# TensorE's order in the first down projection of an attention and bilinear feed-forward kernel, taken from the source

## Chip, cores and metric

The kernel runs on one core of one Trainium2 chip, as one launch. The metric is the device time of that launch in microseconds (us), read as the median of several runs. TensorE (PE) does the matrix products, VectorE (DVE) and ScalarE (ACT) read PSUM and do the elementwise work, GpSimd (POOL) does a little of it, and SyncE (SP) and ScalarE issue the DMA transfers.

## What is computed

The reference computes attention with a causal window of 128 keys and a linear bias, joins the heads, and sends the result through a bilinear feed-forward block. q, k and v have 8 batches, 8 heads, 576 positions and 64 channels; the block's weights are 512 by 1536, twice, and 1536 by 512.

```
scores = scale * np.matmul(q, k.transpose(0, 1, 3, 2))
...
scores = np.where(mask, scores + bias[None], -1000000000.0)
attn = np.exp(scores - max) ; attn = attn / (sum + 1e-09)
attn_out = np.matmul(attn, v)
x = attn_out.transpose(0, 2, 1, 3).reshape(B * S, H * D)
a = x @ w_a
b = x @ w_b
return (a * b @ w_out)
```

## The kernel before, in words

The weights reach the core as 64-bit words and are turned into a pair of 16-bit tiles, a high part and a low part. Almost every product is made of three 16-bit products (high by high, high by low, low by high) in one PSUM bank. `up_weights` (lines 166 to 203) does this for w_a and w_b. `down_weights` (205 to 233) does it for w_out: `convert` (lines 132 to 135, DVE), a square and a sum, a scale, and at the end for each of the 12 row blocks f one ACT copy (line 231) and one DVE subtraction (line 232), which write the tile `wdn`. Both are generators, joined in the chain `weights`; each `next` emits one step.

The batches run in a pipeline: while PE does the feed-forward products of batch b, the attention of batch b + 1 is done in between. `attention()` (line 667) is a generator of seven sections for each of four head pairs, and `Pace.along` (line 987) calls its sections at a set rate along the feed-forward steps. In a pair's turn stand `scores` (line 369: products `sc_ps`, line 380 for batch 1 and 384 later; a DVE pass, line 388; an ACT exponential, line 389), `normalize` (393: ACT line 405 and DVE line 406 write the probabilities into the tile `phl`), `transpose_probs` (409: one transposing DMA on SP's queue, line 411, from `phl` to the tile `pT`), and one pair later `pv` (510: 42 products `x_ps`, line 507, from `pT` and `vhl`). `split_qk` (333) begins with a small product `qtot` (line 337) for the pair after. `phl` is one tile without copies, so the next `normalize` waits until the transposing DMA has read it.

The feed-forward of batch 0 is emitted in `first_batch` (1019). `first_up` (785) makes the 12 hidden blocks f, each of four `up_ps` groups that ACT (line 792) and DVE (line 794) empty. `first_down` (813) then makes the output. For the first half t = 0 of the tokens it goes through f, and for each f through the four output blocks e, with three products each (line 818) into four open PSUM banks `dn_ps`, one for each e. For t = 1 it goes through e, and through f inside. All the banks named `up_ps` and `dn_ps` come from a cycle of five (lines 57 to 62), so a bank can be written only when the one five places earlier in the cycle has been read.

What sets the order: the whole is built under a scheduler that puts each engine's instructions into an order of its own, by a forecast of when they are ready. An engine named in `tc.manual_schedule` is left out: its instructions keep the order in which the source emits them. For the first batch this holds for SP alone (line 1034). For batches 1 to 7 it holds for PE alone (line 1038).

Of the kernel before, what the change touches and what calls it, by code (L numbers as in the profile page):

```python
# [46 lines left out]
def attention_then_bilinear_ffn(ctx: ExitStack, tc: tile.TileContext, qT, kT, vP, w_a, w_b, w_out, rel, slopes2, outT):  # L47
# [11 lines left out]
    def bank(name):  # L59

        pl = next(banks)
        return pl.tile([P, 512], F32, tag="ef" if pl is ps_ef else "ch", name=name)
# [103 lines left out]
    def up_weights():  # L166

        sq, rest, hi, ps = {}, [], [], None  # L170
        for f in range(NF + 2):
            conv = convert(f) if f < NF else iter(())
            next(conv, None)
            n = f - 1
            if 0 <= n < NF:
                if n % 2 == 0:
                    ps = ps_at.tile([P, 512], F32, tag="at", name="wn_ps")
                up_norms(n, sq.pop(n), ps)
                if n + 3 < NF:
                    load_weights(n + 3, (w_a[n + 3], w_b[n + 3]), sp)  # L180
                else:
                    k = 2 * (n + 3 - NF)
                    load_weights(n + 3, (w_out[k], w_out[k + 1]), sp)
            yield
            next(conv, None)
            if rest:
                rest.pop(0)()
            if 0 <= n < NF and n % 2:
                up_scales(n // 2, ps)
                hi += [(k, m) for k in (n - 1, n) for m in range(2)]  # L190
            yield
            if hi:
                rest.append(split_up(*hi.pop(0)))
            yield
            if f < NF:
                sq[f] = squares(f)
            if hi:
                rest.append(split_up(*hi.pop(0)))
            if rest:
                rest.pop(0)()  # L200
            yield
        for _ in range(len(rest)):
            rest.pop(0)()
# [575 lines left out]
    states, started, first_reads, last_read, last_main, last_bias = {}, {"down": -1}, [None], [None], [None], [None]  # L779


    def new_hidden():
        return work.tile([P, 2, HT], F32, tag="rc", name="rc", bufs=3)

    def first_up(st, h):

        late = []
        hid = {}

        def keep(f, t, m, ps):  # L790
            if m == 0:
                act.copy(hid[f][:, t, :], ps[:, 0:HT])
            else:
                vec.scalar_tensor_tensor(out=hid[f][:, t, :], in0=hid[f][:, t, :], scalar=st.g, in1=ps[:, 0:HT], op0=ALU.mult, op1=ALU.mult)
                if t:
                    halve(hid.pop(f), f, h, pool if f >= NF // 2 else vec)

        for f in range(NF):
            hid[f] = new_hidden()
            for t in range(2):  # L800
                for m in range(2):
                    ps = bank("up_ps")
                    terms(ps, (f, 3 if m else 0), B12 if t else 0, True, False)
                    terms(ps, (f, 2 if m else 1), 2 if t else 1, False, True)
                    late.append((f, t, m, ps))
                    if len(late) > 2:
                        keep(*late.pop(0))
                    yield
        for x in late:
            keep(*x)  # L810
        yield

    def first_down(b, oi, h):

        started["down"] = b
        def products(ps, f, e, t):
            for n, (wi, hi) in enumerate(((0, 0), (0, 1), (1, 0))):
                pe.matmul(ps[:, 0:HT], wdn[:, f, wi, e * P:(e + 1) * P], h[:, f, t, hi, :], start=(f == 0 and n == 0), stop=(f == NF - 1 and n == 2))  # L818

        def out(ps, e, t, o):  # L820
            with tc.high_priority(offset=PRIO):
                if e % 2:
                    vec.tensor_scalar(out=o, in0=ps[:, 0:HT], scalar1=oi, scalar2=None, op0=ALU.mult)
                else:
                    last_main[0] = act.activation(o, ps[:, 0:HT], AF.Copy, scale=oi)
            act.dma_start(outT[e * P:(e + 1) * P, b * S + t * HT:b * S + (t + 1) * HT], o)

        pss = [bank("dn_ps") for _ in range(NE)]
        for f in range(NF):
            for e in range(NE):  # L830
                products(pss[e], f, e, 0)
            yield
        more = new_hidden()
        for e in range(NE):
            out(pss[e], e, 0, row() if e < 2 else more[:, e - 2, :])
        for e in range(NE):
            ps = bank("dn_ps")
            for f in range(NF):
                products(ps, f, e, 1)
                if f % 4 == 3:  # L840
                    yield
            out(ps, e, 1, row())

    def row():
        return work.tile([P, HT], F32, tag="row", name="row", bufs=2)
# [115 lines left out]
    def out_scale(st):  # L961

        oi = small.tile([P, 1], F32, tag="oi", name="oi")
        vec.tensor_scalar(out=oi, in0=st.g, scalar1=smin, scalar2=so, op0=ALU.mult, op1=ALU.mult)
        vec.tensor_scalar(out=oi, in0=oi, scalar1=st.sv, scalar2=st.sv, op0=ALU.mult, op1=ALU.mult)
        vec.reciprocal(oi, oi)
        return oi

    def weave(main, *sides):

        for n, _ in enumerate(main):
            for side, a, z, steps in sides:
                if a <= n < z:
                    for _ in range((n + 1 - a) * steps // (z - a) - (n - a) * steps // (z - a)):
                        next(side, None)
# [24 lines left out]
    weights = chain(up_weights(), down_weights())  # L1000
# [4 lines left out]
    h = hid.tile([P, NF, 2, 2, HT], F16, name="h")  # L1005
# [8 lines left out]
    att = Pace(attention())  # L1014
# [4 lines left out]
    def first_batch():  # L1019
        st = states[0]  # L1020
        weave(att.along(first_up(st, h), 49, 3.2), (weights, 0, 40, 50))
        weave(att.along(first_down(0, out_scale(st), h), 24, 5.15), (weights, 0, 12, 12))
        for _ in weights:
            pass

    def batch(b):
        plain, fast = ways[b]
        n = 4 * len(plain) + 7 * len(fast)
        weave(att.along(up(states[b], h, plain, fast), n, NPAIR * b + 4), *((spread, *x) for x in quota[b][0]))
        weave(att.along(down(b, out_scale(states[b]), h, plain + fast), 48, NPAIR * b + 6), *((spread, *x) for x in quota[b][1]))  # L1030
        if b + 1 < B:
            assert b + 1 in states

    with tc.manual_schedule(engines=SP):
        first_batch()


    with tc.manual_schedule(engines={mybir.EngineType.PE}):
        for b in range(1, B):
            batch(b)  # L1040

# [39 lines left out]
```

## Time and profile before

| | |
|---|---|
| median of 3 runs | 992.15 us (991.67 to 992.97) |
| the profiled execution's own time | 989.81 us |
| its span | 988.0 us |
| PE busy | 962.1 us (97%) |
| DVE, ACT, POOL busy | 669.0, 635.6, 255.3 us |
| first down projection's products (line 818) | 288, from 153.5 to 200.2 us |

The span is what the trace covers; the execution's own time is 1.8 us longer. In a row of the timeline the first number is the start, the second the length of the merged group, then engine, line, operation, written tile and read tiles, partitions by elements, and a count; brackets at the end give how long the engine stood idle before it and what released it. Matmuls overlap, so the rate of a group is read from the starts of the group and of the next one.

### The profile page before, as it was taken

To read this page: it belongs to the slowest core of one execution; us is meant where nothing else is said; L and a number is where in the kernel's file an instruction comes from. 1 tells how busy PE (TensorE), PEld (TensorE's weight loads), DVE (VectorE), ACT (ScalarE), POOL (GpSimd) and SP (SyncE) were. 2 spreads that over 40 slices of the span, in tenths; PEclk is the share of its full clock that TensorE was granted. 3 is DMA by queue.
4 is the path that set the end of the run, shared out by engine and by line. 5 is a ranking of instruction groups with operands and counts; after the bars stand their busy time and mean duration, and the time that the engine had idled before them with its cause. 6 is when DMAs were issued, how large, how long until landed. Compare 5 with 4: busy or idle time off the path is not lost.

```text
span 988.0 us, 23867 instructions
## 1 busy us (share of the span) xinstructions
PE 962.1 (97%) x9339; PEld 748.9 (76%) x9339; DVE 669.0 (68%) x1867; ACT 635.6 (64%) x1729; POOL 255.3 (26%) x309
## 2 busy tenths in 40 slices
PE   7899999999999999999999999999999999999998
PEld 5567777677777777777777777777777777877776
DVE  5979998668688657777778677757776576514520
ACT  5977769667676667766767766777667766413321
POOL 1211122032546313541225222211232012311100
PEclk8999999999999999999999999999999999999999
DMA  8434753664337234463345362373245432200001
GB/s 333 168 126 172 231 154 67 151 158 92 80 74 183 68 69 87 107 172 75 68 92 121 120 118 65 87 191 84 59 84 117 133 74 38 55 34 5 1 13 36
DMA packets 148432, 102.82 MB, mean 104 GB/s; under 512 B 120032, under 2 KB 128352, under 8 KB 147296
## 3 DMA queue, kind: packets, MB, share of 16 engines
q1 hardware_dynamic: 138816, 91.77, 38.2%
q10 hardware_dynamic: 9504, 9.54, 3.0%
q8 instruction: 73, 1.20, 0.5%
q14 instruction: 39, 0.32, 0.1%
HBM read 48.33 MB, written 9.44 MB: 58 GB/s over the span
## 4 chain that ended last, share of the span: by engine, by line
PE 69%; DVE 12%; ACT 7%; DMA 7%; issue 3%; POOL 1%; SPq 0%; ACTq 0%; DVEq 0%
PE ch L856 19%; PE dn_ps L952 18%; PE p L856 14%; PE up_ps L856 9%; PE x_ps L507 4%; DMA v<-in_vP 4%; PE sc_ps L384 3%; DVE phl L406 2%; PE dn_ps L818 2%; ACT t L389 1%; DVE wsum L135 1%; DVE xs L442 1%; ACT phl L405 1%; DVE wsum L134 1%; DMA qk<-in_kT 1%
## 5 line engine op out<-in xcount | busy, mean ns | idle before, releaser
L856 PEld LDWEIGHTS <-wup 128*128 128x128 f16 x3072 | 296.3, 98 | 82.0 <-issue 5.7
L952 PE MATMUL dn_ps<-h,wdn 128*128 128x288 f16 x2016 | 254.4, 286 | 0.0
L952 PEld LDWEIGHTS <-wdn 128*128 128x128 f16 x2016 | 193.9, 98 | 52.0 <-issue 0.2
L856 PE MATMUL up_ps<-xs,wup 128*128 128x288 f16 x1536 | 194.6, 286 | 1.1 <-ACT rc L867 0.8
L856 PEld LDWEIGHTS <-wsum 128*128 128x128 f16 x1152 | 111.7, 98 | 32.0 <-issue 2.5
L911 POOL TENSOR_TENSOR rc<-rc,row 128x288 f32<-128x288 f32 x64 | 62.3, 974 | 279.8 <-DVE row L909 263.9
L389 ACT ACTIVATE t<-t,mn 128x192 f32<-128x192 f32 (+2 forms) x252 | 107.2, 427 | 24.5 <-DVE mn L388 24.4
L856 PE MATMUL ch<-xs,wup 128*128 128x288 f16 x768 | 115.0, 286 | 0.5 <-ACT row L893 0.5
L856 PE MATMUL p<-xs,wup 128*128 128x288 f16 x768 | 115.1, 286 | 0.0
L406 DVE SCALAR_TENSOR_TENSOR phl<-t,rin,phl 128x192 f16<-128x192 f32 (+2 forms) x252 | 104.6, 454 | 15.3 <-ACT phl L405 15.1
L856 PE MATMUL ch<-xs,wsum 128*128 128x288 f16 x768 | 111.5, 286 | 1.1 <-ACT rc L881 1.1
L848 ACT CAST h<-rc 128x576 f16<-128x576 f32 x96 | 64.1, 668 | 69.1 <-DVE rc L916 37.2
L405 ACT ACTIVATE phl<-t,rin 128x192 f16<-128x192 f32 (+2 forms) x252 | 88.9, 425 | 25.3 <-DMA pT<-phl 12.7
L849 DVE TENSOR_TENSOR h<-rc,h 128x576 f16<-128x576 f32 x90 | 69.5, 772 | 30.5 <-ACT h L848 29.7
L388 DVE CUSTOM_DVE_ANT_0 t<-sc_ps,bias,neg 128x192 f32<-128x192 f32 (+2 forms) x216 | 73.9, 389 | 7.6 <-PE sc_ps L384 7.5
L957 ACT ACTIVATE row<-dn_ps,oi 128x288 f32<-128x288 f32 x56 | 27.6, 493 | 55.9 <-PE dn_ps L952 55.9
L893 ACT ACTIVATE row<-ch,g 128x288 f32<-128x288 f32 x64 | 31.8, 497 | 48.9 <-PE ch L856 48.9
L442 DVE TENSOR_TENSOR xs<-v,xs 128x576 f16<-128x576 f32 x52 | 47.8, 935 | 21.4 <-ACT xs L441 21.3
L888 DVE TENSOR_TENSOR rc<-p,rc 128x288 f32<-128x288 f32 x64 | 29.1, 454 | 44.3 <-PE p L856 34.7
L365 POOL TENSOR_SCALAR bias<-rel_sb,ninv,sl_sb 128x192 f32<-128x192 f32 x24 | 20.0, 832 | 147.8 <-DVE mn L388 129.8
L856 PE MATMUL p<-xs,wsum 128*128 128x288 f16 x384 | 57.5, 286 | 0.0
L436 POOL TENSOR_TENSOR xq<-xq,sq 128x576 bf16<-128x576 bf16 x22 | 29.2, 1325 | 75.7 <-ACT sq L435 75.7
(155 smaller groups left out, 1386.1 us busy)
## 6 DMA issues: line engine op xcount, KB each, us to landing
v<-in_vP SPq DMA_DIRECT2D x8, 1280.0 KB, 6.2
out<-row ACTq DMA_DIRECT2D x62, 144.0 KB, 1.8
qk<-in_qT SPq DMA_DIRECT2D x28, 288.0 KB, 4.0
qk<-in_kT SPq DMA_DIRECT2D x28, 288.0 KB, 4.4
wdn<-in_w_a SPq DMA_DIRECT2D x12, 512.0 KB, 5.1
wdn<-in_w_b SPq DMA_DIRECT2D x12, 512.0 KB, 6.1
wdn<-in_w_out SPq DMA_DIRECT2D x12, 512.0 KB, 4.6
qst<-qkh SPq DMA_DIRECT2D x24, 144.0 KB, 2.7
```

Of the source, the lines that this page charges most:

```text
L388: vec.tensor_tensor_reduce(out=t[:, c:c + w], in0=ps[:, c:c + w], in1=o.bias[:, WIN - w:WIN], scale=-0.125 if o.b == 1 else o.neg, scalar= ...
L389: act.activation(t[:, c:c + w], t[:, c:c + w], AF.Exp, bias=o.mn[:, n:n + 1], scale=-1.0, accum_out=o.sm[:, n:n + 1])
L405: act.activation(phl[:, 0, pc:pc + w], e, AF.Copy, scale=s)
L406: vec.scalar_tensor_tensor(out=phl[:, 1, pc:pc + w], in0=e, scalar=s, in1=phl[:, 0, pc:pc + w], op0=ALU.mult, op1=ALU.subtract)
L442: vec.tensor_tensor(out=xs[:, n, 1, :, :], in0=src, in1=xs[:, n, 0, :, :], op=ALU.subtract)
L507: last = pe.matmul(xp[oc // 512][64 * h:64 * h + 64, o0:o0 + w], vt[0:rows, c:c + 64], probs(pt, rows, blocks, h), start=(n == 0 and first ...
L848: act.copy(h[:, f, :, 0, :], hid)
L849: eng.tensor_tensor(out=h[:, f, :, 1, :], in0=hid, in1=h[:, f, :, 0, :], op=ALU.subtract)
L856: pe.matmul(ps[:, 0:HT], w[:, wi, k, :], xs[:, b, xi, k, :], start=(first and n == 0), stop=(last and n == len(ks) - 1), skip_group_check= ...
L893: last_read[0] = last_main[0] = act.activation(mid, ch, AF.Copy, scale=st.g)
L911: pool.tensor_tensor(out=x0, in0=x0, in1=mid, op=ALU.mult)
L952: pe.matmul(ps[:, 0:HT], wdn[:, f, wi, e * P:(e + 1) * P], h[:, f, t, hi, :], start=(m == 0 and n == 0), stop=(m == NF - 1 and n == 2))
```

## The change

The call of `first_down` is taken out of `first_batch`, where its steps and twelve steps of `weights` were woven together under the scheduler. What is left of `weights` is now emitted before it, and `first_down` is emitted after it, in the section in which PE's order is that of the source. The rate at which attention is called along it is the same. SP, which kept the source's order in this stage, is now ordered by the scheduler there.

```diff
     def first_batch():
         st = states[0]
         weave(att.along(first_up(st, h), 49, 3.2), (weights, 0, 40, 50))
-        weave(att.along(first_down(0, out_scale(st), h), 24, 5.15), (weights, 0, 12, 12))
         for _ in weights:
             pass
...
     with tc.manual_schedule(engines={mybir.EngineType.PE}):
+        for _ in att.along(first_down(0, out_scale(states[0]), h), 24, 5.15):
+            pass
         for b in range(1, B):
             batch(b)
```

No instruction is added or taken away; all engines keep their order up to the first product of `first_down`, and PE's order is the same again from the 2111th row of its program on. In between the rows move. The number behind a name tells apart the buffers of one tile name.

First place: PE, at the end of the first hidden block f = 0 of `first_down`. `dn_ps_2116` and `dn_ps_2117` are now the banks of output blocks e = 2 and e = 3. Now stands there:

```order
L818 MATMUL dn_ps_2116<-h_787,wdn_122 128x288
L818 LDWEIGHTS wdn_122
L818 MATMUL dn_ps_2117<-h_787,wdn_122 128x288 [waits Activation_49]
L818 LDWEIGHTS wdn_122
L818 MATMUL dn_ps_2117<-h_787,wdn_122 128x288
L818 LDWEIGHTS wdn_122
L818 MATMUL dn_ps_2117<-h_787,wdn_122 128x288
L337 LDWEIGHTS ones16_73 [waits DVE_49]
L337 MATMUL qtot_2142<-both_2042,ones16_73 128x2 [waits PE_49]
```

The fourth bank is opened by the tenth product of `first_down`, and a wait for ACT stands on it. Before, the fourth bank was called `dn_ps_2096`, and its first product stood here, behind 62 other products of `first_down`, `qtot` and eight score products:

```order
L818 MATMUL dn_ps_2094<-h_787,wdn_122 128x288
L818 LDWEIGHTS wdn_122
L818 MATMUL dn_ps_2095<-h_787,wdn_122 128x288
L818 LDWEIGHTS wdn_122
L818 MATMUL dn_ps_2095<-h_787,wdn_122 128x288
L818 LDWEIGHTS wdn_122
L818 MATMUL dn_ps_2096<-h_787,wdn_122 128x288 [waits Activation_49]
```

The same wait moved from the 63rd product of the stage to the 10th.

Second place: PE, at the first products of probabilities and values of the stage (pair 2 of batch 1; `pT_1991` is its transposed probabilities). Now:

```order
L818 LDWEIGHTS wdn_122
L818 MATMUL dn_ps_2117<-h_787,wdn_122 128x288
L380 MATMUL sc_ps_2166<-qkl_1463,qkh_1462 64x192 x4
L507 LDWEIGHTS vhl_2086
L507 MATMUL x_ps_2176<-pT_1991,vhl_2086 64x128 [waits DMAHW4_49]
```

Before:

```order
L818 LDWEIGHTS wdn_122
L818 MATMUL dn_ps_2095<-h_787,wdn_122 128x288
L818 LDWEIGHTS wdn_122
L818 MATMUL dn_ps_2095<-h_787,wdn_122 128x288
L507 LDWEIGHTS vhl_2086
L507 MATMUL x_ps_2157<-pT_1991,vhl_2086 64x128 [waits DMAHW4_49]
```

Of the products of `first_down`, 104 stood ahead of this wait for the transposing DMA before, and 24 stand ahead of it now. The score products `sc_ps_2166` were ahead of it in both.

Third place: ACT, from the last copies of `wdn` in its block of ten on; this is one piece of the difference. The row `L792` is ACT's last reading of an `up_ps` bank, and `L326` is the sum of squares that waits for a load of q and k.

```order
 L792 COPY rc<-up_ps 128x288
-L231 ACTIVATE wdn<-wsum,ratio 128x512
-L389 ACTIVATE t,sm<-t,mn 128x192 x2
-L435 ACTIVATE sq<-v 128x576
-L231 ACTIVATE wdn<-wsum,ratio 128x512
+L389 ACTIVATE t,sm<-t,mn 128x192 x2
+L435 ACTIVATE sq<-v 128x576
+L231 ACTIVATE wdn<-wsum,ratio 128x512 x2
```

Everything up to `L792` stands as it did, ten copies of `wdn` among it, and the two copies left come a little later. Further down, `L326` of the next pair moves ahead of four copies into `phl` (line 405), and the four squares of the next values (line 282) stand in one block. On DVE too the last two `phl` rows of pair 2 (line 406) have the same ten subtractions of line 232 ahead of them. On SP the load of the next values (line 273) moves ahead of a transposing DMA and of two moves of q and k (lines 354 and 355).

## The prediction

> **What bounds the kernel now.** The page comes first: which engine fills the span.
>
> ```profile
> span 988.0 us, 23867 instructions
> PE 962.1 (97%) x9339; PEld 748.9 (76%) x9339; DVE 669.0 (68%) x1867; ACT 635.6 (64%) x1729; POOL 255.3 (26%) x309
> ```
>
> PE is busy for 97% of the span; the whole span holds 25.9 us in which it is not. The change takes no work from PE, so it can win only idle time, and it can lose any amount. The second view is the table by stretches of time around the first down projection (columns: us, then busy time of PE, PEld, DVE, ACT, POOL, then clock, DMA share, GB/s).
>
> ```profile
> 125.00:150.00 25.00, 21.41 (x235) 16.67 (x233) 23.79 (x56) 18.61 (x50) 6.55 (x4) 1.00 0.56 148
> 150.00:175.00 25.00, 24.80 (x252) 18.60 (x253) 21.49 (x69) 22.29 (x57) 4.78 (x5) 1.00 0.40 85
> 175.00:200.00 25.00, 22.57 (x237) 17.55 (x235) 13.15 (x46) 14.28 (x42) 1.78 (x2) 1.00 0.71 148
> 200.00:225.00 25.00, 24.15 (x224) 18.86 (x222) 16.80 (x60) 17.86 (x55) 10.31 (x16) 1.00 0.55 140
> 350.00:988.00 638.00, 631.33 (x6076) 496.61 (x6073) 394.33 (x1119) 383.23 (x1039) 154.58 (x161) 1.00 0.36 80
> ```
>
> From 150 to 175 PE is idle for 0.2 us, from 175 to 200 for 2.4. The third view, PE's waits from 140 to 400 us (total, times, longest), names them:
>
> ```profile
> PE wtot L103 <- DVE c L102: 2.4, 1, 2.4
> PE x_ps L507 <- DMA pT<-phl: 2.4, 1, 2.4
> PE sc_ps L380 <- issue: 1.4, 1, 1.4
> PE sc_ps L384 <- DVE mn L388: 1.2, 2, 0.8
> PE qtot L337 <- DVE both L329: 1.2, 1, 1.2
> PE up_ps L856 <- ACT rc L867: 0.8, 1, 0.8
> ```
>
> The waits of `wtot` and of the 1.4 us stand ahead of the first down product, where no engine's order changes. So the stage to be reordered holds one wait, 2.4 us for a transposed `pT`. The fourth view is PE's timeline of that stage:
>
> ```profile
> 153.47 0.90 PE L818 MATMUL dn_ps<-h,wdn 128*128 128x288 f16 x6
> 154.30 0.87 PE L380 MATMUL sc_ps<-qkl,qkh 64*64 64x192 f32 x8
> 155.10 4.22 PE L818 MATMUL dn_ps<-h,wdn 128*128 128x288 f16 x33
> 159.16 0.17 PE L337 MATMUL qtot<-both,ones 128*128 128x2 bf16 x1
> 160.32 7.89 PE L818 MATMUL dn_ps<-h,wdn 128*128 128x288 f16 x63
> 168.14 1.54 PE L507 MATMUL x_ps<-pT,vhl 128*64 128x128 f16 x42
> 169.61 0.87 PE L380 MATMUL sc_ps<-qkl,qkh 64*64 64x192 f32 x8
> ...
> 183.93 0.25 PE L507 MATMUL x_ps<-pT,vhl 128*64 128x128 f16 x2 [2.44 <-DMA pT<-phl]
> ```
>
> Up to 168.14 PE never stands still here: the scheduler has 104 down products ready to fill with. A down product takes 0.125 us (7.82 us from 160.32 to 168.14, by 63), a group of eight score products 0.80 (154.30 to 155.10). What the first `x_ps` and the fourth bank wait for is on the other engines' timelines, ACT, then DVE, then SP, and in the DMA view from 160 to 168 us (last number: us from issue to landing):
>
> ```profile
> 158.17 0.79 ACT L405 ACTIVATE phl<-t,rin 128x192 f16<-128x192 f32 x2
> 160.02 0.38 ACT L792 COPY rc<-up_ps 128x288 f32<-128x288 f32 x1
> 167.46 0.64 ACT L405 ACTIVATE phl<-t,rin 128x64 f16<-128x64 f32 x2 [0.63 <-DMA pT<-phl]
> ```
> ```profile
> 159.84 0.74 DVE L406 SCALAR_TENSOR_TENSOR phl<-t,rin,phl 128x192 f16<-128x192 f32 x2
> ```
> ```profile
> 160.65 4.84 SPq L411 DMA_TRANSPOSE pT<-phl  x1
> ```
> ```profile
> pT<-phl SPq DMA_TRANSPOSE x1, 6.7
> ```
>
> The last `phl` row ends near 160.6, the transposing DMA is issued at 160.65 and lands 6.7 us later, at 167.4. Before, `x_ps` stood at 168.14, just behind it.
>
> **The change part by part.** No instruction comes or goes, and PE's order is new only from 153.47 us to the `qtot` ahead of the second `x_ps`. Three moves have a price.
>
> *The fourth bank, opened by the tenth product.* With five banks in a cycle, the one for e = 3 held the third `up_ps` group of f = 11, and ACT reads it in the L792 row that ends at 160.40. ACT's rows up to there are the same and wait for nothing that PE now does later, so it still ends at 160.40. PE reaches that product at 153.47 + 9 x 0.125 + 0.80 = 155.4 and stands for 5.0 us. Queued behind it is everything on PE.
>
> *`x_ps` of pair 2, moved ahead of 80 down products.* By its place PE would reach it after 24 down products and two score groups: 153.47 + 24 x 0.125 + 2 x 0.80 = 158.1. Its `pT` lands at 167.4. The stall up to there is 9.3 us, and the 5.0 of the fourth bank lie inside it: from 160.4 PE has 15 products left, `qtot` and a score group, 2.8 us, so it stands again from 163.2 to 167.4. Both ends of the DMA rest on ACT's L405 and DVE's L406; ahead of these the order shows the same ten copies and ten subtractions of `wdn`, so the "work on w_out above" moves neither. Term: +9.3.
>
> *The second `x_ps`.* From 153.47 to 183.93 PE did 30.46 - 2.44 = 28.0 us of work, and it is the same work now; PE comes there at 153.47 + 28.0 + 9.3 = 190.8. Is its `pT` there by then?
>
> ```profile
> 176.86 1.16 ACT L326 ACTIVATE qkl<-qk 128x1152 bf16<-128x1152 f32 x1 [2.72 <-DMA qk<-in_kT]
> ```
> ```profile
> 174.65 9.23 DMA pT<-phl
> ```
>
> The first row is ACT's timeline, the second the chain that ended last. ACT's L326 is now queued ahead of four L405 copies of pair 3, and it waits for a load. If that load is as late as before, ACT is through with L326 at 178.0, with four copies at 0.4 (two took 0.79) at 179.6; DVE is half a microsecond behind, and with 9.2 for the DMA `pT` is there near 189.4. That is ahead of 190.8, so the old wait of 2.4 goes: -2.4. Together: +6.9.
>
> *The clock.* Two idle times of 5.0 and 4.2 us with 2.8 us of work between are longer than any that this stage had. What the trace shows of such holes is at its start, and at the two waits of 2.4 (stretches of 3.41 us, laid on the clock's own changes; the first number behind the comma is PE's busy time, the clock stands third from the end):
>
> ```profile
> 8.82:12.23 3.41, 1.45 (x10) 0.73 (x8) 3.17 (x11) 2.17 (x8) 0.07 (x1) 1.00 0.99 404
> 12.23:15.64 3.41, 2.59 (x32) 2.12 (x34) 1.30 (x3) 3.41 (x10) 1.20 (x1) 0.50 1.03 407
> 22.47:25.88 3.41, 1.89 (x16) 0.96 (x14) 3.41 (x13) 2.46 (x8) 0.00 (x0) 1.00 0.94 330
> 25.88:29.29 3.41, 3.41 (x23) 2.68 (x24) 2.83 (x7) 2.15 (x8) 2.21 (x3) 0.50 0.78 284
> 141.92:145.34 3.42, 1.96 (x16) 1.33 (x14) 3.03 (x4) 1.24 (x3) 1.28 (x1) 1.00 0.19 42
> 179.47:182.88 3.41, 2.02 (x21) 1.32 (x19) 0.97 (x8) 1.60 (x7) 0.00 (x0) 1.00 1.08 259
> ```
>
> A stretch with 1.45 or 1.89 us busy was followed by one at a granted clock of 0.50; those with 1.96 and 2.02 were not. An idle time of 5.0 us leaves some stretch at least 2.5 us empty, under 0.9 busy, so the clock should fall. At 0.50 the 2.8 us of work between the stalls take at most 5.6 and still end before 167.4: nothing lost there. What counts is the half clock left at 167.4: none at best, at worst one stretch nearly whole and a second (the one from 12.23, at 0.50 with 2.59 busy, was followed by another at 0.50): 0 to 3.1 us lost, since half of the time at 0.50 is lost. I take 1.5, near half of one stretch, as the place of the stretches is not known. Term: +1.5.
>
> The Trainium skill ("TensorE: Matmul & The Clock Gate", section "What's actually happening") says that the clock halves after a window of about 3.4 us that is idle, and that the windows run freely. By that rule, taken to the letter, 5.0 us need not hold a whole empty window, the clock would mostly stay, and the sum would lack this term. The rows here show falls after stretches 42 and 55% busy, so I go by the rows.
>
> *Behind the stage.*
>
> ```profile
> 215.49 6.04 PE L856 MATMUL up_ps<-xs,wup 128*128 128x288 f16 x48 [0.85 <-ACT rc L867]
> ```
> ```profile
> 202.12 0.58 SPq L273 DMA_DIRECT2D v<-in_vP  x1
> ```
> ```profile
> 208.40 0.74 ACT L282 ACTIVATE vsq<-v 128x640 bf16<-128x640 f32 x1 [1.71 <-DMA v<-in_vP]
> ```
>
> ACT was late at 215.49 because its squares of `v` (L282) stood among its other rows and waited for a load until 208.40, 6.3 us after its issue. Now the load is issued ahead of a transposing DMA and the squares stand in one block, early beside a PE that comes some 8 us later: -0.9, with nothing as the other end. Its own price: the load is now ahead of two moves of q and k (L354, L355) that score products need.
>
> ```profile
> 189.63 2.44 DMA qst<-qkl
> ```
>
> From the score products that set these moves free to the ones that need them stand 72 down products, 9.0 us; the load's 6.3 and a move's 2.4 make 8.7, with two issues and a second move up to some 10.5. So it costs 0 to 1.5; I take 0. The other waits behind (1.2 of `qtot`, 1.2 of `sc_ps`) have the same order around them and stay; at best they go.
>
> Sum: +9.3 - 2.4 + 1.5 - 0.9 = +7.5 us. The profiled execution took 989.81 (span 988.0), so 997.3; the median of the runs is 992.15, 2.3 above it, and with the same shift the median is 999.7 us.
>
> **Rivals.**
>
> *Given back later.* The chain of attention is 2 to 4 us ahead of PE after the stage, so all later waits of the list could shrink: 2.4 for `qtot` and `sc_ps` beside the 0.9, and no clock loss: 9.3 - 2.4 - 0.9 - 2.4 = +3.6, 995.8. For it: those waits are on DVE and ACT. Against: they come after 60 us and more of a pipeline that PE's own order times. Chance 0.10.
>
> *The clock stays at 1.00*, as it did over the two holes of 2.4: +6.0, 998.2. Chance 0.20. By the page of the Trainium skill named above, taken to the letter, this is the likely course.
>
> *A new wait behind.* The half clock takes its full 3.1 and the moves of q and k come late by 1.5: +10.6, 1002.8. Chance 0.12.
>
> *Not slower.* The copies and subtractions of `wdn` emitted above let ACT and DVE reach L792, L405 and L406 earlier than the rows of before say, and `pT` lands by 160.5 instead of 167.4. Then `x_ps` costs at most 2.4, the later wait goes, and the sum is zero or a little under it: 992.1 to 990. It decides at 160.5: the DMA would have to be issued by 153.8, 6.9 us earlier. Against it: the same ten copies stand ahead of these rows on ACT, which is busy for 22.29 of the 25 us from 150 on. Chance 0.05. That the order does not change is excluded by its rows.
>
> **How the numbers follow.** The forecast has the remaining 0.53, at 999.7. The range reaches from the first rival's 995.8 to 1003.0, just above the third's: outside are the not-slower case and ends of two bounds at once. A measurement of this kernel tells about 0.2%, 2 us, from no change; every case but the last is above that. Faster 0.02, same 0.03, slower 0.95.
>
> **What would show it.** Right: PE's timeline with a wait of some 5 us on the tenth down product for ACT's `rc`, one of 1.5 to 4 us on `x_ps` for the DMA to `pT` near 167.4, no wait on the next `x_ps`, and a clock of 0.50 somewhere between 158 and 171. Wrong: `x_ps` starts before 164; or the second `x_ps` still waits; or the sum of PE's idle time grows by less than 4 us. If the clock's row reads 1.00 throughout, the term of 1.5 is wrong and the rest may stand.

## The result, and the profile after

The changed kernel takes 998.77 us (median of 7 runs, 997.49 to 1002.27) against 992.15 for the kernel before (7 runs, 989.50 to 995.00): a ratio of 1.007, 95% interval 1.0048 to 1.0093. It is slower by 0.7%, which lies within the forecast range; the forecast was 999.7. The profiled execution took 1000.83 us with a span of 998.9 at a mean granted clock of 0.988; that of before had 989.81, 988.0 and 0.995. So the two traces stand 11.0 us apart and the medians 6.6. Part of what follows is about that gap.

The page first, of the changed kernel.

```profile
span 998.9 us, 23865 instructions
PE 967.2 (97%) x9339; PEld 752.8 (75%) x9339; DVE 671.5 (67%) x1867; ACT 636.8 (64%) x1729; POOL 255.7 (26%) x309
```

PE does the same 9339 products and is busy 5.1 us longer with them; the rest of the 10.9 us by which the span grew is idle time. Work that lasts longer without having grown points at the clock. The table by stretches, with the columns of the prediction, says where:

```profile
150.00:175.00 25.00, 17.71 (x168) 12.74 (x163) 20.73 (x59) 20.00 (x51) 4.73 (x4) 0.85 0.42 89
175.00:200.00 25.00, 25.00 (x258) 19.74 (x257) 12.62 (x47) 15.19 (x44) 2.29 (x3) 1.00 0.49 113
200.00:225.00 25.00, 22.91 (x197) 17.47 (x195) 15.46 (x56) 15.83 (x50) 4.97 (x6) 0.93 0.75 170
```

From 150 to 175 PE had 252 products before and has 168 now, and its clock fell from 1.00 to 0.85. From 175 to 200 it makes up the 2.4 us of the old wait. From 200 to 225 it loses again, 27 products fewer at 0.93, in a stretch for which the forecast had a small gain. PE's waits from 140 to 400 us name the causes:

```profile
PE dn_ps L818 <- ACT rc L792: 4.8, 1, 4.8
PE x_ps L507 <- DMA pT<-phl: 2.5, 1, 2.5
PE wtot L103 <- DVE c L102: 2.5, 1, 2.5
PE sc_ps L384 <- DMA qkh<-qkh: 1.6, 1, 1.6
...
PE sc_ps L384 <- DMA qkl<-qkl: 0.5, 1, 0.5
```

The first two are the predicted stalls. The last two, score products that wait for moved q and k, are new, and the 0.8 for `up_ps` is gone. In PE's timeline:

```profile
153.66 0.41 PE L818 MATMUL dn_ps<-h,wdn 128*128 128x288 f16 x2
...
160.61 0.84 PE L818 MATMUL dn_ps<-h,wdn 128*128 128x288 f16 x3 [4.78 <-ACT rc L792]
161.24 0.21 PE L337 MATMUL qtot<-both,ones 128*128 128x2 bf16 x1
161.31 2.98 PE L818 MATMUL dn_ps<-h,wdn 128*128 128x288 f16 x12
164.22 0.87 PE L380 MATMUL sc_ps<-qkl,qkh 64*64 64x192 f32 x8
167.59 2.77 PE L507 MATMUL x_ps<-pT,vhl 128*64 128x128 f16 x42 [2.50 <-DMA pT<-phl]
...
191.98 1.51 PE L507 MATMUL x_ps<-pT,vhl 128*64 128x128 f16 x42
...
207.80 0.22 PE L384 MATMUL sc_ps<-qkh,qst 128*64 128x64 f16 x2 [1.64 <-DMA qkh<-qkh]
208.47 0.27 PE L384 MATMUL sc_ps<-qkl,qst 128*64 128x64 f16 x2 [0.45 <-DMA qkl<-qkl]
...
240.77 1.54 PE L507 MATMUL x_ps<-pT,vhl 128*64 128x128 f16 x42
```

The same third `x_ps` in the timeline of before:

```profile
229.81 1.54 PE L507 MATMUL x_ps<-pT,vhl 128*64 128x128 f16 x42
```

Three distances hold the whole difference between the two traces. From the first down product to the second `x_ps`: 30.46 us before (153.47 to 183.93), 38.32 now. From there to the third `x_ps`: 45.88 before, 48.79 now. From the third `x_ps` to the end of the span: 758.2 and 758.1. So all of it lies in these two parts, +7.86 and +2.91, and nothing is won or lost behind 240 us. The experiments are read by the same two distances.

### The profile page after: what moved, and what is told of

Its sections match the earlier page's. It is cut to its first block, busy times and chain, and to the rows that moved or that the text cites. A ratio compares the mean times of both kernels' runs of the same rounds, so it can differ in the third digit from the quotient of the medians.

```text
span 998.9 us, 23865 instructions
## 1 busy us (share of the span) xinstructions
PE 967.2 (97%) x9339; PEld 752.8 (75%) x9339; DVE 671.5 (67%) x1867; ACT 636.8 (64%) x1729; POOL 255.7 (26%) x309
## 4 chain that ended last, share of the span: by engine, by line
PE 73%; DVE 11%; ACT 7%; DMA 5%; issue 2%; POOL 0%; ACTq 0%; SPq 0%; DVEq 0%
PE ch L856 19%; PE dn_ps L952 18%; PE p L856 14%; PE up_ps L856 12%; PE x_ps L507 4%; PE sc_ps L384 3%; PE dn_ps L818 3%; DVE phl L406 2%; DMA v<-in_vP 1%; ACT phl L405 1%; DVE wsum L135 1%; ACT t L389 1%; DVE xs L442 1%; DVE wsum L134 1%; DVE t L388 1%
## 5 line engine op out<-in xcount | busy, mean ns | idle before, releaser
L405 ACT ACTIVATE phl<-t,rin 128x192 f16<-128x192 f32 (+2 forms) x252 | 88.7, 425 | 23.4 <-DMA pT<-phl 10.6
```

The source lines that it names most:

```text
L405: act.activation(phl[:, 0, pc:pc + w], e, AF.Copy, scale=s)
```

## The experiments

**Theory.** TensorE's order costs two nested stalls and the fall of the clock that they bring; the later waits come from SP, which the change also hands to the scheduler. **Rivals:** the work on w_out that now stands above; the new waits coming from PE's late place; the clock alone; and the attention sections standing at wrong places rather than the order as such.

All runs in one table: the ratio of the run's times to those of the kernel before on the same chip, with its 95% interval (the ratio of the two medians can differ from it by 0.001), and the two distances in the run's own trace.

| run | ratio | first down product to second `x_ps` | second to third `x_ps` | both |
|---|---|---|---|---|
| before | 1 | 30.46 | 45.88 | 76.34 |
| changed | 1.0070 [1.0048, 1.0093] | 38.32 | 48.79 | 87.11 |
| changed again (e7) | 1.0080 [1.0062, 1.0099] | 38.38 | 48.84 | 87.22 |
| e1, weights above only | 1.0001 [0.9988, 1.0013] | 30.39 | 45.57 | 75.96 |
| e2, SP by source too | 1.0061 [1.0044, 1.0079] | 38.11 | 44.84 | 82.95 |
| e9, e2 with squares behind `phl` | 1.0057 [1.0039, 1.0075] | 38.38 | 44.85 | 83.23 |
| e3, fourth bank late | 1.0097 [1.0074, 1.0121] | 40.91 | 48.87 | 89.78 |
| e6, warm | 1.0076 [1.0057, 1.0094] | 37.14 | 50.38 | 87.52 |
| e11, warm and SP by source | 1.0056 [1.0039, 1.0073] | 36.92 | 45.36 | 82.28 |
| e4, attention late | 1.0157 [1.0140, 1.0173] | 38.68 | 52.40 | 91.08 |
| e5, sections placed by hand | 1.0090 [1.0074, 1.0107] | 36.09 | 50.12 | 86.21 |
| e8, e5 with squares behind `phl` | 1.0050 [1.0033, 1.0067] | 32.92 | 49.80 | 82.72 |
| e10, before with a later second `x_ps` | 1.0012 [0.9997, 1.0027] | 31.03 | 47.67 | 78.70 |

In e4, e5, e8 and e10 the second `x_ps` stands behind another number of products, so for these only the last column can be set beside the others. In e5 and e8 even that needs a correction: 24 products of `up_ps` more than elsewhere stand ahead of their third `x_ps`, 3.0 us at 0.125 each. Less these, e5 has 83.2 and e8 79.7.

**e1: the half of the change that moves the weights' work.** PE stays under the scheduler, and the steps of `weights` stand above `first_down`.

```diff
-        weave(att.along(first_down(0, out_scale(st), h), 24, 5.15), (weights, 0, 12, 12))
         for _ in weights:
             pass
+        for _ in att.along(first_down(0, out_scale(st), h), 24, 5.15):
+            pass
```

> One part of the change alone: the work on w_out's words stands above the first down projection in the source, and PE's order there is left to the scheduler as before. The instructions of all engines then stand in the order of the kernel before, row for row. Theory (the price is PE's order): 1.000 of before, within 0.2%. Rival (the weights above delay something): there is no row by which it could. Besides, its profile is a second look at the program of before: the mean granted clock of most executions of before was 0.991 to 0.993, below the 0.995 of the profiled one, so a stretch at 0.50 behind one or both of the 2.4 us waits is expected, with 1 to 3 us more than the profiled execution of before.

Measured: 991.79 us against 991.30, and a stage that is 0.4 us off that of before. In the traces of both, the instructions of every engine have the same order. So this half of the change does nothing by itself, and the first rival falls. The run is also twelve more executions of what is before's program, and its profiled one was 2.6 us longer than before's, with one stretch of half clock more. That stretch did not come where it was expected, behind a wait of 2.4 us (the clock of e1 reads 1.00 from 125 to 200 us), but early. From 40 to 60 us, in before and then in e1:

```profile
40.00:60.00 20.00, 17.80 (x223) 12.03 (x220) 18.15 (x43) 17.95 (x49) 4.37 (x9) 1.00 0.16 55
```
```profile
40.00:60.00 20.00, 17.79 (x193) 11.74 (x193) 18.82 (x45) 17.39 (x49) 4.72 (x10) 0.91 0.24 89
```

The busy time is the same, 30 products fewer are done. One such stretch (3.41 us at 0.50) costs up to 1.7 us, by estimate half of its length, and lowers the mean clock by 0.0017. So it explains at most 1.7 of the 2.6 us.

**e2: SP keeps the source's order too.** In its trace SP has the order of before, and PE that of the changed kernel. ACT and DVE, which the scheduler orders, still differ from before in some places, and from the changed kernel in others.

```diff
-    with tc.manual_schedule(engines={mybir.EngineType.PE}):
+    with tc.manual_schedule(engines={mybir.EngineType.PE, mybir.EngineType.SP}):
         for _ in att.along(first_down(0, out_scale(states[0]), h), 24, 5.15):
             pass
+    with tc.manual_schedule(engines={mybir.EngineType.PE}):
         for b in range(1, B):
```

> The changed kernel, with SyncE's queue too in the source's order during the first down projection, so that the next values are loaded behind the two moves of q and k and the transposing DMA, as in the kernel before. Theory (most of the time is PE standing at two early waits): the waits of 4.8 us on the fourth bank and on x_ps until pT lands near 167.6 stay as in the changed kernel, and x_ps of pair 3 starts near 192; only the wait of 1.6 + 0.5 us for qkh and qkl at 207.8 goes, with the half clock behind it of up to 1.7 us. So 2 to 4 us less than the changed kernel, and in place of that the old 0.85 us at up_ps may come back: about 995 to 997.5 us, 1.003 to 1.006 of before. Rival (SyncE's order is what costs the time): back to 992, 1.000 of before, and the two early waits shrink.

Measured: 996.55 us. PE's waits from 140 to 300 us in e2:

```profile
PE dn_ps L818 <- ACT rc L792: 4.7, 1, 4.7
PE wtot L103 <- DVE c L102: 3.0, 1, 3.0
PE x_ps L507 <- DMA pT<-phl: 2.7, 1, 2.7
PE sc_ps L384 <- DVE mn L388: 0.4, 1, 0.4
```

Both predicted stalls stay; the waits for moved q and k are gone, with the same PE order. So those are not PE's late place, but SP's order. In SP's timeline of the changed kernel the load of v stands ahead of two moves, and the DMA view from 195 to 215 us (last number: us from issue to landing) shows what that does:

```profile
198.27 0.53 SPq L273 DMA_DIRECT2D v<-in_vP  x1
199.42 0.46 SPq L354 DMA_DIRECT2D qkh<-qkh  x1
200.23 0.46 SPq L355 DMA_DIRECT2D qkl<-qkl  x1
```
```profile
v<-in_vP SPq DMA_DIRECT2D x1, 1280.0 KB, 9.0
...
qkh<-qkh SPq DMA_DIRECT2D x1, 144.0 KB, 8.2
qkl<-qkl SPq DMA_DIRECT2D x1, 144.0 KB, 8.2
```

In e2 the load is issued at 210.06, behind the transposing DMA, as it is behind it in before; there, from 185 to 200 us, the same two moves took

```profile
qkh<-qkh SPq DMA_DIRECT2D x1, 144.0 KB, 2.9
qkl<-qkl SPq DMA_DIRECT2D x1, 144.0 KB, 3.5
```

That SP's order makes these waits is shown; that it is the load of v within it is read from these rows. In the traces of e3, e6 and e7, which have the load at the same place, the two moves took 7.4 to 8.3 us. SP's share is 4 us in the traces (87.11 and 87.22 against 82.95 and 83.23). By the ratios it is 0.9 to 2.3 us (1.0070 to 1.0080 against 1.0061 to 1.0057, on 991), and these intervals overlap, so in the times SP's share is not clear of noise. The larger part, 5.6 to 6.0 us by the ratios of e2 and e9, comes with PE's order. What the other order on ACT and DVE adds to it is not measured apart, beyond the one rule of e9 below; but the ends of the two stalls stand where they did, measured from the first down product: ACT's L792 ends 6.93 us behind it in before and 6.90 in the changed kernel, and the transposing DMA is issued 7.18 and 7.19 us behind it.

**e7: the changed kernel once more**, beside e6, e8 and e9 on one chip.

> The changed kernel once more, on the same chip and beside the same runs of the kernel before as the other three. All theories: 1.005 to 1.009 of before; its waits at the fourth bank (4.8), at x_ps (until pT lands, 1.5 to 4.2 by what the clock leaves of the time between) and at the scores behind the load of v (1.6 + 0.5) again.

Measured: 1000.24 us, ratio 1.0080, both distances within 0.1 us of the first trace. PE waited 2.83 us at the first `x_ps`, within the expected 1.5 to 4.2.

**e3: the fourth bank opened late.** The products of e = 3 are held back until the sixth hidden block, so that PE no longer waits for ACT at the tenth.

```diff
         for f in range(NF):
-            for e in range(NE):
+            for e in range(NE - 1):
                 products(pss[e], f, e, 0)
+            for g in range(6) if f == 5 else (f,) if f >= 6 else ():
+                products(pss[NE - 1], g, NE - 1, 0)
             yield
```

> The changed kernel, with the products into the fourth bank (e = 3) held back until the sixth hidden block, so that no early product waits for ACT's L792. Theory (the fourth bank's wait lies inside the wait for pT): the 4.8 us wait vanishes from the list, the wait of x_ps grows from 2.5 to about 10 us, x_ps starts at 167.4 to 167.7 as before, and the time is that of the changed kernel within 2 us (997 to 1001). The one long idle time instead of two may leave the clock at half at another place. Rival (the bank's wait adds to the other): 4 to 5 us less than the changed kernel, 994.

Measured: 999.12 us, ratio 1.0097. The bank's wait is gone, and `x_ps` waits so much longer:

```profile
169.74 2.77 PE L507 MATMUL x_ps<-pT,vhl 128*64 128x128 f16 x42 [9.46 <-DMA pT<-phl]
```

`x_ps` starts 14.63 us behind the first down product (155.11 to 169.74), against 13.93 in the changed kernel: taking the bank's wait away brings it no earlier, so the bank's stall is nested in that of `x_ps`, as the prediction had it. The first distance is even 2.6 us longer: `x_ps` starts 0.7 us later, 6 down products more stand behind it (0.75 us), and the rest fits the clock, which in this trace reads 0.50 until 175.44, 5.7 us behind the start of `x_ps`, and in the changed kernel until 170.94, 3.35 us behind it.

**e6 and e11: PE kept busy in the stalls.** 34 and 26 products by a tile of zeros go into the open bank of e = 0, where they add nothing; they stand ahead of the tenth down product and ahead of the score group before `x_ps`. e6 is the changed kernel with these, e11 is e2 with them.

```diff
+    zero16 = const.tile([P, P], F16, name="zero16")
+    pool.memset(zero16, 0.0)
...
+        def idle_work(n):
+            for _ in range(n):
+                pe.matmul(pss[0][:, 0:HT], zero16, h[:, 0, 0, 0, :], start=False, stop=False)
+
         for f in range(NF):
             for e in range(NE):
+                if f == 0 and e == 3:
+                    idle_work(34)
                 products(pss[e], f, e, 0)
+            if f == 1:
+                idle_work(26)
             yield
```

> The changed kernel, with products by a tile of zeros added to the first open bank where PE would stand idle: 34 ahead of the tenth down product and 26 ahead of the score products before x_ps (4.3 and 3.3 us at 0.125 us each). They add nothing to the result and take nothing from the waits, which end when ACT's L792 ends and when pT lands. Theory with a clock term (idle stretches halve the clock, and the half clock left behind the landing of pT costs 1 to 3 us): the granted clock stays 1.00 from 153 to 175 us, x_ps takes 1.5 us instead of 2.8, and the time from the first down product to the x_ps of pair 3 falls from 38.3 us to 36.6 or a little more; the later wait for qkh and qkl stays. Time 1 to 3 us under that of the changed kernel beside it. Rival (the clock term is nothing): no difference in that stage, x_ps still at 2.8 us or the same start of the x_ps of pair 3.

> The changed kernel with the products by zeros in PE's two early idle times and with SyncE in the source's order. The kernel with these products alone kept the clock at 1.00 and won 1.2 us up to the x_ps of pair 3, but stood longer behind it for the load of v. Theory (that gain was given back at the later wait): here the later wait is gone, so from the first down product to the x_ps of pair 3 it takes 37.1 us and from there to the next x_ps 44.9, together 82.0 against 83.0 to 83.2 in the two kernels with SyncE in the source's order; 1.004 to 1.006 of before. Rival (the clock is worth nothing): 83 or more.

Measured, e6: 997.96 us, ratio 1.0076. By the medians that is 2.3 us under the changed kernel beside it (e7), by the ratios 0.4, and the intervals overlap: no gain is shown in the time. In the trace the clock reads 1.00 from 150 to 175, the waits shrink to 0.65 and 1.06, and from the first `x_ps` to the second PE takes 23.09 us (168.57 to 191.66), where the changed kernel took 24.39. So the fallen clock costs 1.3 us in the stage; the first distance falls to 37.14, where 36.6 or a little more was expected.

```profile
150.00:175.00 25.00, 22.04 (x217) 16.70 (x218) 21.32 (x65) 20.83 (x51) 5.45 (x6) 1.00 0.38 78
```
```profile
168.57 1.54 PE L509 MATMUL x_ps<-pT,vhl 128*64 128x128 f16 x42 [1.06 <-DMA pT<-phl]
...
191.66 1.54 PE L509 MATMUL x_ps<-pT,vhl 128*64 128x128 f16 x42
```

But behind that PE reaches the moves of q and k earlier:

```profile
209.01 0.22 PE L386 MATMUL sc_ps<-qkh,qst 128*64 128x64 f16 x2 [2.77 <-DMA qkh<-qkh]
209.66 0.22 PE L386 MATMUL sc_ps<-qkl,qst 128*64 128x64 f16 x2 [0.43 <-DMA qkl<-qkl]
```

The wait grew from 1.64 to 2.77, and the clock fell behind it too (0.93 from 200 to 225): in the trace the gain is given back. In e11, without those waits, the two distances are 36.92 and 45.36, a stage of 82.28 beside e2's 82.95. The time (997.49, ratio 1.0056) can't be told from e2's. "The clock alone" falls: with the clock at 1.00 and SP's order as before, the change still costs 5.6 us by that ratio.

**e4: attention called late.** Its sections begin only at the seventh step of `first_down`, so that 72 products more stand ahead of the first `x_ps`.

```diff
-        for _ in att.along(first_down(0, out_scale(states[0]), h), 24, 5.15):
-            pass
+        start = att.at
+        for n, _ in enumerate(first_down(0, out_scale(states[0]), h), 1):
+            att.to(start + (5.15 - start) * max(n - 6, 0) / 18)
```

> The changed kernel, with attention called along the first down projection only from its seventh step on, so that x_ps of pair 2 stands behind 96 down products instead of 24; the fourth bank is still opened by the tenth product. Theory: PE still stands 4.8 us for ACT's L792, reaches x_ps near 172, behind the landing of pT at 167.5, and does not wait there. qtot comes 10 us later than in the changed kernel, so what hangs on it (the moves of q and k, the scores of batch 2) comes later, and a new wait of 0 to 4 us for these scores or for the next pT is possible. Against before: +4.8, up to 1.7 for the clock, -2.4 if the next x_ps does not wait: 994 to 998 us. Rival (the order of the other engines carries the price, not the place of x_ps): as the changed kernel, 999.

Measured: 1006.04 us, a miss by 8 us and more. The stall at `x_ps` is gone, as expected. The rest of the attention, pressed into what is left of the stage, pays for it:

```profile
173.41 1.54 PE L507 MATMUL x_ps<-pT,vhl 128*64 128x128 f16 x42
...
198.25 0.37 PE L384 MATMUL sc_ps<-qkh,qst 128*64 128x192 f16 x2 [2.50 <-DVE mn L388]
212.05 0.27 PE L384 MATMUL sc_ps<-qkl,qst 128*64 128x64 f16 x2 [5.31 <-DMA qkl<-qkl]
```

The chains from scores to moves have their own length, and a place that is late for one consumer is early for the next.

**e5 and e8: sections placed by hand.** PE and SP by source, the bank late as in e3, and each attention section called at a step chosen to stand where the scheduler had it. e8 adds one rule: ACT's squares of the next q and k (line 326) are issued behind the last copy into `phl`. e9 is e2 with that rule alone.

```diff
+    with tc.manual_schedule(engines={mybir.EngineType.PE, mybir.EngineType.SP}):
+        due = {1: 3, 8: 5, 9: 7, 11: 8, 12: 9, 14: 10, 17: 11, 19: 12, 20: 13, 22: 14, 24: 15}
+        for n, _ in enumerate(first_down(0, out_scale(states[0]), h), 1):
+            if n in due:
+                att.to(3 + due[n] / 7)
     with tc.manual_schedule(engines={mybir.EngineType.PE}):
-        for _ in att.along(first_down(0, out_scale(states[0]), h), 24, 5.15):
-            pass
```
```diff
-            act.activation(phl[:, 0, pc:pc + w], e, AF.Copy, scale=s)
+            last_phl[0] = act.activation(phl[:, 0, pc:pc + w], e, AF.Copy, scale=s)
...
-            with behind():
+            with tc.issue_after(last_phl[0].ins) if b == 2 and p == 0 else behind():
                 nxt = squares(i + 1)
```

> PE and SyncE in the source's order in the first down projection, with the fourth bank's products held back to the sixth hidden block and attention's sections placed by hand: qtot behind step 1, x_ps of pair 2 and the score products behind step 8, x_ps of pair 3 behind step 17. Theory: by its place PE reaches the first x_ps near 167.2 and waits 0 to 0.5 us; it reaches the second near 184.3, some 0 to 0.4 us behind the landing at 183.9 in the kernel before, so the old wait of 2.4 us goes too. So 1 to 2.5 us less than before, 989.5 to 991.5 us, a ratio of 0.997 to 0.999. Rival (a PE order that is written by hand costs by itself, through the other engines' order): 2 us or more above before, 994 or more.

> The kernel with hand-placed sections and the late fourth bank, with one more rule: ACT's sum of squares for the next pair (L326), which stood 4.35 us for a load of k ahead of the last four copies into phl, is issued behind these copies. Theory (the second x_ps waits for pT because L326 holds up phl): the transposing DMA is issued near 175.6 instead of 180.1, pT lands near 185, the wait of 3.6 us on the second x_ps falls to 0 to 0.6, and the half clock behind it goes, so 3 to 5 us less than the hand-placed kernel: 994 to 996, 1.004 to 1.006 of before. If the waits at up_ps and at sc_ps behind 215 us come from the same lateness, they shrink too, down to 991. Rival (the landing is set by the DMA queue's traffic): pT still lands near 188.8, and the time stays at 999.

> The changed kernel with SyncE in the source's order and the same rule, ACT's L326 behind the copies into phl. Theory: the second x_ps does not wait in the changed kernel, so an earlier pT is worth nothing there: the time of the kernel with SyncE in the source's order, 1.005 to 1.007 of before, while the transposing DMA is issued some 2 us earlier. Rival (ACT's order carries part of the price): 2 us or more less than that.

Measured, e5: 999.24 us, a miss by nearly 8 us, on the side of its rival. The first `x_ps` no longer waits, but the second waits 3.55. ACT's timeline in e5 has the reason, and that of e8 what the rule does:

```profile
176.93 1.16 ACT L326 ACTIVATE qkl<-qk 128x1152 bf16<-128x1152 f32 x1 [4.35 <-DMA qk<-in_kT]
...
178.10 1.48 ACT L405 ACTIVATE phl<-t,rin 128x192 f16<-128x192 f32 x4
```
```profile
175.15 1.49 ACT L405 ACTIVATE phl<-t,rin 128x192 f16<-128x192 f32 x4 [0.92 <-DVE rin L402]
177.11 1.16 ACT L326 ACTIVATE qkl<-qk 128x1152 bf16<-128x1152 f32 x1 [0.47 <-DMA qk<-in_kT]
```

A sum of squares that waits 4.35 us for a load stood ahead of the copies that the transposing DMA needs. With the order turned, the second `x_ps` waits 0.36, the first distance falls by 3.17, and the time to 995.93, as expected. Measured, e9: 997.16 us, ratio 1.0057, the same as e2's 1.0061, since there the second `x_ps` had not waited. So in these runs the wait that the prediction feared in its third step exists only when PE comes to it early. What is left in e8 are small new waits: 1.05, 0.69 and 1.89 at `up_ps` and 0.75 at `sc_ps` make 4.4 us between the second and third `x_ps`, and 0.89 at `qtot`, 0.79 at `sc_ps` and 0.36 at `x_ps` stand ahead of these. Together they are 6.4 us, where before had 3.3 (2.44 and 0.85); that accounts for 3.1 of the 3.4 us by which the corrected stage is longer. Behind the third `x_ps`, where the changed kernel loses nothing, e8 loses 3.8 us (758.96 for 758.2 less 3.0): it waits 2.67 more at `sc_ps` at 274.8, and the clock reads 0.50 from 274.42 to 277.84. So with both stalls gone the sections placed by hand still cost 0.5%, and no run here shows what order would cost nothing short of the scheduler's. This rival stays partly open.

**e10: the kernel before, its second `x_ps` 24 products later.** This tests whether the 2.4 us wait that the change removes is worth anything where nothing else is changed. PE is under the scheduler.

```diff
-        weave(att.along(first_down(0, out_scale(st), h), 24, 5.15), (weights, 0, 12, 12))
+        start = att.at
+        for n, _ in enumerate(first_down(0, out_scale(st), h), 1):
+            place = start + (5.15 - start) * n / 24
+            late = {15: 4.42, 16: 4.42, 17: 4.5, 18: 4.57, 19: 4.71, 20: 4.8, 21: 4.86}
+            att.to(min(place, late.get(n, place)))
+            if n <= 12:
+                next(weights, None)
```

> The kernel before, with PE's order left to the scheduler, and attention's sections placed so that the x_ps of pair 3 stands behind 24 more down products; nothing else on PE moves. Theory (waits move with the place of x_ps): the wait of 2.4 us for pT goes, the products moved ahead fill it, and the x_ps starts 0 to 0.7 us later than in the kernel before (183.9 in its profile). Behind it ACT and DVE have less time for the rest of the stage, so up to 1 us may come back at the scores or at up_ps. 0.9975 to 0.9995 of before, up to 4 us if the clock fell behind that wait. Rival (the wait comes back whole at the next place that needs attention): 1.000.

Measured: 992.09 us, ratio 1.0012, a miss: no gain, as its rival had it. The wait went, and came back at another place:

```profile
186.88 1.51 PE L507 MATMUL x_ps<-pT,vhl 128*64 128x128 f16 x42
...
203.45 0.18 PE L337 MATMUL qtot<-both,ones 128*128 128x2 bf16 x1 [1.06 <-DVE both L329]
...
218.56 7.71 PE L856 MATMUL up_ps<-xs,wup 128*128 128x288 f16 x48 [2.27 <-ACT rc L867]
```

In e1, the same program but for that place, the first of these waits is absent and the second is 0.5. ACT stood 1.69 us for the load of v at 212.77, with its copy out of `up_ps` behind it, and the clock fell once behind that wait (0.93 from 200 to 225). PE was ahead of its suppliers, and the idle time moved down the line.

No version was faster than the kernel before.

## Why the prediction was right, step by step

**The fourth bank** was forecast at 5.0 us and measured 4.78. That it is nested in the next stall is shown by e3.

**The first `x_ps`** was forecast to start 13.93 us behind the first down product (153.47 to 167.4) and did, 153.66 to 167.59. It waited 2.50 and not 4.2 because the 15 products, `qtot` and score group between the stalls ran at half clock for most of it and took 4.48 us (160.61 to 165.09) in place of 2.8; they still ended before the DMA, as forecast.

**The second `x_ps`** came at 191.98 for a forecast of 190.8 + 1.5, and without a wait. ACT's L326 stood only 0.55 us for its load; the transposing DMA was issued at 179.63 and took 7.0 us, so `pT` was there some 5 us early, where the forecast had 1.4; e9 shows that more of it is worth nothing.

**The clock** term was 1.5 us and e6 gives 1.3. It is above all the first `x_ps` at 2.77 us instead of 1.54. The forecast had taken half of a stretch because the place of the stretches was not known; that its size came out so well is in part luck. The stretches of 3.41 us, laid on the clock's own changes in the trace of the changed kernel (PE's busy time behind the comma, the clock third from the end):

```profile
143.64:147.05 3.41, 0.96 (x11) 0.59 (x10) 2.61 (x8) 2.40 (x7) 0.00 (x0) 1.00 0.01 2
147.05:150.46 3.41, 3.41 (x50) 2.59 (x48) 3.01 (x15) 3.41 (x9) 1.30 (x2) 0.50 0.00 0
157.29:160.70 3.41, 0.09 (x1) 0.09 (x1) 3.41 (x8) 3.41 (x13) 0.00 (x0) 1.00 0.00 0
160.70:164.11 3.41, 3.41 (x16) 2.01 (x15) 3.03 (x12) 3.41 (x9) 1.27 (x1) 0.50 0.67 128
164.11:167.53 3.42, 0.98 (x10) 0.58 (x9) 3.42 (x5) 2.00 (x3) 1.75 (x1) 1.00 1.01 191
167.53:170.94 3.41, 3.35 (x45) 3.06 (x45) 3.20 (x10) 3.21 (x12) 0.00 (x0) 0.50 0.28 62
205.08:208.49 3.41, 1.32 (x13) 0.78 (x12) 0.38 (x2) 1.09 (x3) 0.00 (x0) 1.00 1.28 114
208.49:211.90 3.41, 3.41 (x27) 2.41 (x27) 1.09 (x8) 2.87 (x9) 0.00 (x0) 0.50 1.17 279
```

Four holes, four stretches at 0.50 behind them, and in each case the stretch ahead held some products. The Trainium skill ("TensorE: Matmul & The Clock Gate", section "What's actually happening") has the clock fall after an idle window of some 3.4 us. By the letter at most the second of the four falls would have come, behind 0.09 us busy. The stretches with 0.96, 0.98 and 1.32 us busy speak against the letter and for the prediction's reading of the rows of before.

**Behind the stage** is the step that failed in size: by the distances of the traces, the first part was forecast at +8.4 and measured +7.86, and this one at -0.9 and measured +2.91. The forecast had -0.9 for the `up_ps` wait and 0 (0 to 1.5) for the load of v ahead of the moves of q and k. The wait of 0.85 did go. But the moves took 8.2 us and not the 2.4 of an undisturbed one, PE waited 1.64 + 0.45, and the clock fell behind that, up to 1.7 by estimate: -0.85 + 2.09 + 1.7 = +2.9, beside the +2.91 of the second distance. The bound of 1.5 had let the load and the moves land one behind the other; it had left out that a wait of 2 us in an otherwise full stretch can bring half a clock with it. The third rival had the late moves too, with 1.5 us for them and 3.1 of clock behind the first `x_ps`. Measured were 2.09, and 1.3 of clock there with up to 1.7 behind the moves. So its sum of +10.6 lies nearer to the traces than the forecast's, though half of its clock loss fell at another place.

**The shift to the median** covered the missing term. Trace to trace the forecast was +7.5 and the measured time +11.0. The forecast median then added 2.3 us, as the profiled execution of before lay below its median; the changed kernel's profiled execution lies 2.06 above its own. So the forecast median came within 1 us of the measured one in part by luck. Some of the 11.0 is before's own trace: against the 992.41 of e1, the same program, the two traces of the changed kernel (1000.83 and 1000.37) are 8.4 and 8.0 longer. But the stage itself grew by 10.8 to 11.3 us in every pair of these traces, while the intervals of the ratios give 4.8 to 9.2 us for the changed kernel and 6.1 to 9.8 for e7. The part ahead of the stage, which has the same instructions, differs by up to 3 us from trace to trace (the first down product starts at 152.82 in e7 and at 155.95 in e1); that adds noise to a pair of traces, but no difference between the kernels.

The granted clock may be a reason. Before's profiled execution had a mean of 0.995; of 23 executions of before beside e1, 15 had 0.991 or 0.993, one or two half-clock stretches more than in the trace. The changed kernel's first 7 had 0.986 to 0.991. Before's two holes of 2.4 us did not halve the clock in its trace, nor in e1's; in other executions they may. But the mean clock does not settle it: among the executions at 0.993 the times of those 23 run from 989.32 to 992.89. So why the ratios give less than the stages of the traces stays open.

**The rivals.** "Given back later" did not come: the waits of `qtot` and `sc_ps` behind the stage stayed at 1.2 each. "The clock stays" fell by the rows above. "Not slower" by the weights' work standing above fell twice: in e1 that work moves no row, and in the changed kernel the transposing DMA was issued at 160.85, for a forecast of 160.65.

## What to carry to other kernels

When an engine is put into source order, price every queue that the same scope hands over: here the scope also took SP out of source order, and a 1.28 MB load slipped ahead of two small moves. A stall that ends at a fixed arrival is not shortened by removing another stall nested in it; price the last arrival. On an engine that is 97% busy, a wait that is taken away ahead of its suppliers tends to come back further down (e4, e6, e10), so look up who is late next before counting it as a gain.

## What the runs showed of the hardware

The granted clock halves, for one stretch of 3.41 us or for several, behind a stretch that need not be idle. In the traces of before and after up to 260 us, stretches at full clock with up to 1.9 us of PE busy were followed by 0.50 (0.09, 0.96, 0.98, 1.32, 1.45 and 1.89 among them), and those with 1.95 or more were not. The other traces show that this bound is not sharp. In all thirteen, every stretch at full clock with up to 1.50 us busy was followed by 0.50 and none with more than 2.00, but in between both came: 1.62 in e7 (153.37 to 156.78) and 1.52 in e8 (223.22 to 226.63) were not followed by 0.50, and 2.00 in e5 (7.87 to 11.28) was. So a hole of 2.4 us halves the clock or not by where it falls on the stretches: the hole at `wtot` did in the trace of the changed kernel (147.05 above) and did not in that of before, with the same instructions around it.

A transfer of 144 KB issued 1 to 2 us behind a 1.28 MB load took 8.2 us to land in the changed kernel (7.4 to 8.3 in e3, e6 and e7), and 2.9 to 3.5 in before, where no load of that size was ahead.
